# A new order, engines and buffer places for all 908 steps of a fused linear-attention and gated-MLP kernel

## The chip, the cores and the metric

The kernel runs on one core of a Trainium2 chip. The metric is the device time of one execution in microseconds. Five engines work side by side, each through its own list of instructions in order: PE (TensorE, matmuls; its weight loads are shown as PEld), DVE (VectorE), ACT (ScalarE), POOL (GpSimd) and SP (SyncE, which here only issues DMAs). They meet through semaphores.

## What is computed

An attention layer with a decaying state, and behind it a gated MLP whose gate is a cosine:

```python
batch, n_heads, seq, head_dim = (4, 8, 768, 48)
f = 1.0 / (1.0 + np.exp(-f_logit))
for t in range(S):
    state = f[:, :, t, :, None] * state + np.einsum('bhd,bhe->bhde', k[:, :, t], v[:, :, t])
    y[:, :, t] = np.einsum('bhd,bhde->bhe', q[:, :, t], state)
x = y.transpose(0, 2, 1, 3).reshape(B * S, H * D)      # 3072 x 384
h = x @ w_in                                           # 384 x 2048
g = h * np.cos(h)
out = g @ w_out                                        # 2048 x 384
```

## The kernel before

The sequence is cut into 12 pairs of chunks (three pairs to a batch entry, 256 tokens each), and the MLP into 12 units of 256 tokens; unit n works on the output of pair n. All of it is written as a graph of 908 named steps, each of which issues one or a few instructions on one engine. A name is a kind, the number of the pair or unit, and a part:

- f, k, q, v: loads of a pair's inputs (SP, 384 KB; pairs 0 and 1 in halves of 192 KB). w0.i and w1.i: a quarter of w_in and of w_out (768 KB), with wc0.i and wc1.i, the casts to bf16.
- ex, ln, fx, fy, ad, qa, ka: logs of the gates and what goes with them; cum: their running sum on PE; eb and ei: its exponentials on ACT.
- qm and km: q and k times these (lines 492, 503 and 507), on DVE or POOL. tq and tk: their transposes, on PE for pairs 0 to 3 (lines 569 and 575, with the copy qkt out of PSUM) and as DMA transposes issued by SP for the rest (tqn.0, tqn.1, line 558).
- sc: scores on PE (line 595), am: their mask on DVE (line 599, reads the whole of the scores' two PSUM banks). vb and vt: v in bf16 and placed for the products. ps: the outer products of the state (lines 616 and 626), st and sz: the state's sum and decay on DVE (lines 647 and 652). y and yi: the output inside the chunk and from the state (line 680). xe: its copy to bf16.
- hm.js: one eighth of x @ w_in for unit m (line 728, two steps to a block j of 1024 PSUM columns), co: the cosine on ACT (line 733), g: the product on DVE (line 710), which is the last to read the block's two PSUM banks. or.s: a quarter of g @ w_out for row block r (line 744), ot: its copy out of PSUM, out: its DMA.
- zf0 to zf35: 36 matmuls of zeros (line 302) whose result is not used. zqk, zsp, zvt: memsets of buffers.

Nothing is scheduled by the framework. The string ORDER lists all steps; each engine issues its own in that order. A word such as "g0.2:V" or "h0.21:T0" gives the step, the engine (T is PE, V DVE, S ACT, G POOL, Y SP) and the numbers of the buffers that it takes: for PE's results a PSUM bank from 0 to 7 (steps with 1024 columns take two), for others a slot of their pool. A buffer is free for its next user when the last reader of the value in it has run; the semaphore waits follow from that and from what a step reads. SP too runs in order: a DMA whose buffer is not free, or a store whose data is not there, holds up all behind it.

Of the kernel before, what the change touches and what calls it, by code (L numbers as in the profile page):

```python
# [45 lines left out]
tq0.1:T7 ei1.0:S k1.0:Y0 sc0.0:T2 q1.0:Y0 v1.0:Y0 v1.1:Y vb0.0:V1 eb1.0:S0 cum3:T0 vb0.1:V km0.1:G
am0.0:V1 q1.1:Y ei3:S k1.1:Y zf21:T4 zf22:T4 zf23:T6 tk0.1:T qkt0.1:V0 vs0:T4 ps0.1:T6,2 ps0.0:T
vt0.1:V2 eb3:S1 sz0.00:V3 ex1.1:S zf24:T3 zf25:T3 sc0.1:T0 qm1.0:G1 w0.0:Y2 sz0.01:V zf26:T3 zf27:T3
zf28:T3 zf29:T3 sj0.1:T w0.1:Y0 am0.1:V0 vt0.0:S ln1.1:S q2:Y2 ex2:S sz0.10:V2 km1.0:V cum1.1:T4
vb1.1:V1 ei1.1:S km1.1:V vb1.0:S tq1.0:T6 yi0:T0 y0:T7 zf30:T3 zf31:T3 zf32:T3 zf33:T3 zf34:T3  # L50
tk1.1:T1 sz0.11:V tk1.0:T eb1.1:S qm1.1:V zf35:T4 tq1.1:T qkt1.0:V3 sj1.0:T2 xe0.1:S3 vs1:T4 wc0.0:G
# [6 lines left out]
qkt2.0:S4 h1.20:T qkt2.1:V3 km3.0:G sc2.0:T4 km3.1:G h0.31:T v2:Y0 wc1.3:G tq3.0:T3 am2.0:V0 o0.0:T2
vb2:G2 o1.0:T5 co1.2:S1 w1.2:Y2 co0.3:S0 o3.0:T4 o3.1:T vt2.3:G2 tk3.0:T qkt3.0:S2 ex4:S ln4:S0
g1.2:V fx4:S o1.1:T qm3.1:V tq3.1:T7 tk3.1:T g0.3:V o0.1:T sc3.0:T0 qkt3.1:V0 sc3.1:T6 ad4:G2 v3:Y1  # L60
vb3:G0 o0.3:T o2.0:T3 f5:Y0 o2.1:T vt2.0:S k4:Y2 am3.1:V3 am3.0:V1 fy4:S o2.3:T sc2.1:T6 ps2.0:T0
wc1.2:S ps2.1:T st2.00:V st2.01:V vt2.2:S vt2.1:S o3.3:T vt3.1:G0 q4:Y1 o1.3:T k5:Y0 am2.1:V2 v4:Y1
# [16 lines left out]
out2:Y h4.11:T co4.1:S0 st6.11:V g4.2:V vb7:S1 h5.20:T4 h5.21:T g4.3:V ot6:V0 qm7.0:G tq7.0:Y2
km7.1:G sz6.10:V3 h5.10:T2 co5.2:S2 qm7.1:G tq7.1:Y1 q8:Y2 h5.11:T vt6.0:G o7.2:T0 qa6:G co5.1:S1  # L80
qm6.1:G tq6.1:Y3 o7.3:T vt6.3:S g4.1:V o7.0:T sz6.11:V zsp.0:V g5.2:V0 qm6.0:G vt7.1:G0 sc7.0:T4
vt7.0:G g5.1:V ps7.1:T6,7 ex9:S out5:Y ps7.0:T st7.00:V st7.01:V sz7.01:V1 o9.2:T1 sz7.00:V st7.10:V
o9.0:T o7.1:T am7.0:V3 o9.1:T ln9:S0 fy9:S out6:Y st7.11:V sz7.10:V0 fx9:S sz7.11:V ex8:S tq6.0:Y0
o9.3:T vt7.3:G ln8:S1 q9:Y1 k9:Y0 vt7.2:S o8.1:T6 sc6.1:T4 am6.1:V1 sc7.1:T2 vt6.1:G ot9:S0 out9:Y
ad9:G2 cum9:T7 k8:Y2 o8.0:T o8.2:T ad8:G1 cum8:T5 yi7:T1,4 am7.1:V2 y7:T ot7:S3 xe7.1:V0 v8:Y1 fy8:S
qa8:G xe7.0:S sc6.0:T2 eb8:S0 am6.0:V0 o8.3:T k11:Y1 ei8:S2 h7.20:T0 ei9:S1 ka9:G ot8:V0 fx8:S
km9.0:G1 yi6:T5 qa9:G y6:T4 km9.1:G f11:Y3 eb9:S1 qm9.1:G h7.21:T h5.30:T6 h5.00:T2 xe6.0:V3 xe6.1:V
h5.01:T out4:Y h6.00:T4 co7.2:S1 g7.2:V3 co5.0:S2 h5.31:T h6.21:T0 g5.0:V co5.3:S1 g5.3:V vb8:G0
h6.20:T co6.2:S3 h6.01:T co6.0:S1 g6.2:V4 g6.0:V h6.11:T2 h6.10:T h6.31:T6 vt8.1:S0 o11.2:T1
co6.1:S0 v9:Y0 g6.1:V tq9.1:Y2 ka8:G km8.0:G2 qm9.0:G o10.2:T0 out8:Y h6.30:T q11:Y0 co6.3:S1  # L90
h7.10:T4 h7.11:T co7.1:S0 vb9:G1 tq9.0:Y1 o10.3:T o10.1:T g6.3:V o10.0:T o11.1:T qm8.0:G f10:Y2
ex11:S o11.0:T g7.1:V ex10:S ln10:S0 qm8.1:G vt8.0:G vt9.0:S2 ln11:S1 fx11:S out7:Y ot10:V2 sc9.0:T6
v10:Y1 tq8.0:Y0 km8.1:G ps9.1:T0,2 am9.0:V3 sc9.1:T4 am9.1:V1 ps9.0:T sz9.01:V1 sz9.00:V st9.10:V
st9.11:V o12.0:T3 o12.3:T k10:Y0 vt8.3:G o12.1:T o11.3:T ot11:S3 sz9.10:V3 o12.2:T vt9.3:G vt9.1:G
sz9.11:V ad10:G0 fx10:S cum10:T4 eb10:S1 ei10:S0 vt9.2:G tq8.1:Y3 v11:Y2 h7.31:T6 ot12:V0 sc8.0:T0
out12:Y ka10:G km10.1:G1 yi9:T2 y9:T3 xe9.1:V3 h7.30:T am8.0:V1 co7.3:S0 h7.00:T4 g7.3:V o13.1:T2
h7.01:T o13.3:T o13.2:T o13.0:T xe9.0:S vb10:G1 sc8.1:T6 ad11:G1 km10.0:G co7.0:S3 fy11:S g7.0:V
ps8.0:T3 out11:Y ps8.1:T zvt.1:G ps10.1:T0,1 fy10:S ps10.0:T cum11:T4 ei11:S2 am8.1:V3 st8.00:V
st8.01:V sz8.00:V1 o14.2:T5 eb11:S2 sz8.01:V ka11:G vb11:S2 vt8.2:G o14.3:T o14.0:T o14.1:T yi8:T4,7
st10.00:V y8:T qa11:G qm11.0:G2 xe8.0:S1 ot13:V3 km11.1:G h9.21:T2 st10.01:V vt11.2:G2 sz10.00:V2  # L100
h9.20:T xe8.1:V sz10.01:V h8.30:T6 ot14:S0 co9.2:S0 st10.10:V st10.11:V q10:Y2 qm11.1:G sz10.10:V0
qa10:G sz10.11:V g9.2:V1 h8.31:T h8.11:T0 co8.3:S3 h8.21:T4 qm10.1:G tq11.1:Y1 out3:Y g8.3:V4
# [765 lines left out]
```

## Time and profile before

| | |
|---|---|
| time, median of 3 runs | 179.81 us (179.35 to 180.32) |
| the profiled execution | 179.81 us |
| its span, first to last instruction | 177.8 us |
| PE busy | 171.3 us (96%) |
| DVE, ACT, POOL busy | 133.1, 129.8, 98.2 us |
| granted TensorE clock | 1.000 |
| read from and written to HBM | 25.17 MB and 4.72 MB |

The page and the answers of the trace give times in us from the start of the span. A group reads: line, engine, operation, out<-in with the program's buffer names, shapes, count, busy time. In the list of waits a row reads: who waited, for whom, us in total, how often, the longest. In the chain of waits a row is a piece of the path that ended last: its start, its length, what it was. Matmuls are pipelined and their ends are modelled, so neighbours overlap by a little.

### The profile page before, as it was taken

The numbers are of one execution on the slowest core, as the hardware profiler recorded it, in microseconds if no ns is written. First come the engines' busy times: TensorE is split into PE (matmuls) and PEld (weight loads), VectorE is DVE, ScalarE is ACT, GpSimd is POOL, SyncE is SP. The second block draws the span as 40 slices with busy tenths as digits, with TensorE's granted clock in tenths as the row PEclk, the third lists the DMA queues.
The fourth block names the chain that finished last, engine by engine and source line by source line (L and its number), as shares of the span: only waits on it lengthen the run. The fifth ranks groups of instructions, "written<-read, shape, count | busy, mean of one in ns | idle before, by whom it ended". The sixth has DMA issues, their size and how long they took to land.

```text
span 177.8 us, 5968 instructions
## 1 busy us (share of the span) xinstructions
PE 171.3 (96%) x2551; PEld 125.7 (71%) x2554; DVE 133.1 (75%) x208; ACT 129.8 (73%) x177; POOL 98.2 (55%) x125
## 2 busy tenths in 40 slices
PE   7999989999999999999899999999999999999992
PEld 2576768866678867788567886676786767887660
DVE  6299878897696899796997687978878966283710
ACT  3977687759999999778978789989693644464510
POOL 7042569685669989989746988379992000000000
PEclk9999999999999999999999999999999999999999
DMA  4999999999998799997999999991077040000033
GB/s 128 310 307 344 347 352 259 314 307 309 259 243 221 164 245 217 265 232 133 248 173 290 272 204 262 217 264 40 4 162 166 0 177 4 4 12 32 6 130 133
DMA packets 70330, 34.46 MB, mean 194 GB/s; under 512 B 59296, under 2 KB 68768, under 8 KB 70304
## 3 DMA queue, kind: packets, MB, share of 16 engines
q1 hardware_dynamic: 69744, 33.69, 77.8%
q8 instruction: 20, 0.33, 0.8%
q10 hardware_dynamic: 560, 0.39, 0.8%
q14 instruction: 6, 0.05, 0.1%
HBM read 25.17 MB, written 4.72 MB: 168 GB/s over the span
## 4 chain that ended last, share of the span: by engine, by line
PE 87%; DMA 5%; DVE 2%; issue 1%; ACT 1%; SPq 1%; DVEq 0%; ACTq 0%
PE ps L744 34%; PE ps L728 31%; PE ps L680 5%; PE ps L595 4%; DMA out_dram<-ot 3%; PE ps L302 3%; DMA f<-in_f_logit_dram 2%; PE ps L626 1%; DVE g L710 1%; PE ps L569 1%; PE ps L575 1%; PE ps L438 1%; SPq L336 1%; PE ps L424 1%; PE ps L440 1%
## 5 line engine op out<-in xcount | busy, mean ns | idle before, releaser
L710 DVE TENSOR_TENSOR g<-ps,co 128x1024 bf16<-128x1024 f32 x48 | 57.8, 1220 | 18.9 <-ACT co L733 18.1
L744 PE MATMUL ps<-w_out_bf,g 128*128 128x384 bf16 x384 | 68.4, 326 | 0.0
L733 ACT ACTIVATE co<-ps,halfpi 128x1024 bf16<-128x1024 f32 x48 | 52.6, 1112 | 21.6 <-PE ps L728 20.5
L728 PE MATMUL ps<-x,w_in_bf 128*128 128x256 bf16 x576 | 67.4, 273 | 0.0
L728 PEld LDWEIGHTS <-w_in_bf 128*128 128x128 bf16 x576 | 55.4, 98 | 8.5
L744 PEld LDWEIGHTS <-g 128*128 128x128 bf16 x384 | 36.1, 98 | 21.6
L599 DVE TENSOR_TENSOR am<-ps,pmask 128x1024 bf16<-128x1024 f32 x24 | 28.8, 1219 | 5.3 <-PE ps L595 5.0
L787 ACT ACT_TABLE_LOAD x12 | 15.4, 1283 | 1.7 <-PEq L852 1.5
L507 POOL TENSOR_TENSOR qk<-k,bi 128x384 bf16<-128x384 f32 x16 | 16.0, 1000 | 0.6
L507 POOL TENSOR_TENSOR qk<-q,b 128x384 bf16<-128x384 f32 x16 | 15.9, 1001 | 0.6
L197 POOL COPY vt<-vb 64x384 bf16<-64x384 bf16 x27 | 13.5, 501 | 1.3
L410 POOL TENSOR_TENSOR sp<-ls 128x384 bf16<-128x384 f32 x8 | 8.0, 998 | 8.2 <-ACT ls L378 8.1
L197 ACT COPY ot<-ps 128x384 f32<-128x384 f32 (+1 forms) x13 | 5.5, 438 | 9.0 <-PE ps L744 9.0
L197 DVE COPY ot<-ps 128x384 f32<-128x384 f32 (+1 forms) x13 | 6.9, 535 | 6.6 <-PE ps L744 3.5
L302 PE MATMUL ps<-zero 128*128 128x512 bf16 x33 | 10.1, 435 | 1.6 <-DVE zero L203 1.2
L372 ACT ACTIVATE f<-f 128x768 f32<-128x768 f32 (+1 forms) x14 | 10.2, 746 | 1.3 <-DMA f<-in_f_logit_dram 1.3
L595 PE MATMUL ps<-qkt 48*64 48x128 bf16 x384 | 9.4, 220 | 1.4 <-DVE g L710 0.7
L647 DVE TENSOR_TENSOR ps<-ps,sz 128x192 f32<-128x192 f32 x26 | 9.4, 362 | 1.6 <-PE ps L626 0.9
L396 POOL TENSOR_TENSOR k<-k,f 128x384 f32<-128x384 f32 x8 | 8.0, 999 | 4.5 <-DMA k<-in_k_dram 4.5
L595 PEld LDWEIGHTS <-qkt 48*64 48x64 bf16 x384 | 6.3, 106 | 5.1 <-issue 4.3
L197 DVE CAST x<-ps 128x384 bf16<-128x384 f32 x14 | 7.3, 552 | 2.7 <-PE ps L680 2.7
L197 POOL CAST w_in_bf<-g 128x1536 bf16<-128x1536 f32 x4 | 5.9, 1464 | 5.2 <-DMA g<-in_moe_w_in_dram 5.2
(105 smaller groups left out, 189.5 us busy)
## 6 DMA issues: line engine op xcount, KB each, us to landing
out_dram<-ot SPq DMA_DIRECT2D x22, 192.0 KB, 2.6
f<-in_f_logit_dram SPq DMA_DIRECT2D x10, 384.0 KB, 6.7
q<-in_q_dram SPq DMA_DIRECT2D x10, 384.0 KB, 5.3
k<-in_k_dram SPq DMA_DIRECT2D x10, 384.0 KB, 6.7
v<-in_v_dram SPq DMA_DIRECT2D x10, 384.0 KB, 6.1
g<-in_moe_w_in_dram SPq DMA_DIRECT2D x4, 768.0 KB, 8.9
g<-in_moe_w_out_dram SPq DMA_DIRECT2D x4, 768.0 KB, 8.5
q<-in_q_dram SPq DMA_DIRECT2D x4, 192.0 KB, 4.7
```

Of the source, the lines that this page charges most:

```text
L197: (nc.scalar.copy if e == "ACT" else eng(e).tensor_copy)(out=o, in_=i)
L302: G.step(f"zf{i}", ("PE",), lambda e, dump=dump: nc.tensor.matmul(dump.ap, lhsT=zero[:, 0:128], rhs=zero, start=True, stop=True), writes=[ ...
L372: nc.scalar.activation(out=flat(t.ap), in_=flat(t.ap), func=AF.Exp, scale=-1.0)
L507: G.step(f"{nm}{n}.{u}", ("POOL", "DVE") if cut else ("POOL",), lambda e, u=u, j=j, src=src, dec=dec: eng(e).tensor_mul(out=qkp[u][j].ap[: ...
L595: nc.tensor.matmul(o[64 * h:64 * h + 64, r, 2 * a + g, :].rearrange("p (e n) -> p e n", e=2), lhsT=qkv(u)[s, 1, a, g, h, :], rhs=qkv(u)[s, ...
L599: G.step(f"am{n}.{u}", ("DVE",), lambda e, u=u, sc=sc: nc.vector.tensor_mul(out=am[u].ap.rearrange("p r b n -> p (r b) n"), in0=sc.ap.rear ...
L647: G.step(f"st{n}.{g}{r}", ("DVE",), lambda e, r=r, view=view, S0=S0: nc.vector.tensor_add(out=view(), in0=view(), in1=S0.ap[:, :, r, :]), ...
L710: nc.vector.tensor_mul(out=o.rearrange("p b (n e) -> p b n e", e=2), in0=ph.ap.rearrange("p (b e n) -> p b n e", e=2, n=64), in1=co.ap.rea ...
L728: nc.tensor.matmul(ph.ap[:, i * T:(i + 1) * T].rearrange("p (g t) -> p g t", t=C), lhsT=w_in_bf[:, kk, f0:f0 + 128], rhs=xa[:, :, kk, :], ...
L733: G.step(f"co{m}.{j}", ("ACT",), lambda e, ph=ph, co=co: nc.scalar.activation(out=co.ap, in_=ph.ap, func=AF.Sin, bias=halfpi), reads=[ph], ...
L744: nc.tensor.matmul(po.ap[:, 0:DM], lhsT=gT.ap[:, j, i * C:(i + 1) * C], rhs=w_out_bf[:, j, :], start=(po.first and j == 4 * s), stop=(po.f ...
L787: nc.scalar.preload_act_table_set(TABLES[s.table])
```

## The change

ORDER is replaced as a whole, in 78 lines instead of 80, so every line of the new kernel has a number lower by two (line 710 is line 708). No function, no step and no pool size changes; each engine still issues the same kinds of work, PE the same 2554 matmuls. What changes is the order on each engine, the engine of some steps and the buffer of most.

```diff
 ORDER = """
-cqs:G zsp.1:G f0.0:S3 zqk.1:V zsp.2:G f0.1:Y f3:Y0 ex0.0:S ln0.0:S2 ex0.1:S ln0.1:S f1.0:Y1 zqk.2:G
-zvt.2:V q0.0:Y1 k0.0:Y2 cqi:V zf0:T1 zf1:T1 zf2:T1 zf3:T1 zf4:T1 zf5:T1 zf6:T1 zf7:T1 zf8:T2 zf9:T2
...
-h0.21:T0 k3:Y2 g1.1:V3 km2.1:G qm3.0:G2 h0.20:T co1.0:S3 g1.0:V w1.3:Y4 tq2.1:T3 h1.31:T4 h1.30:T
...
+zf9:T2 zf20:T7 zf13:T1 zf28:T4 f0.1:S1 zf15:T3 zqk.1:G f0.0:Y zf2:T1 cqi:V zf16:T2 zf32:T6 ex0.1:S
+zf25:T6 zsp.0:V zf14:T5 zf35:T3 zf24:T2 zf27:T4 ex0.0:S k0.0:Y1 f1.0:Y0 zsp.1:G ln0.0:S1 q1.1:Y2 zqk.0:V
...
+w1.3:Y2 km3.1:G zf10:T6 g1.1:V h0.20:T tq2.0:T2 tk2.0:T km3.0:V v2:Y2 h1.20:T6 co1.3:S1 wc1.0:G g1.3:V
...
```

Three places, as the instructions stand on their engine.

DVE, from the second product g of unit 0 to the mask of a scores block of pair 3; g_154, g_157 and g_155 are the products g of units 0 and 1, qk_124, qk_125 and qk_123 the results of qm and km of pairs 2 and 3. Before:

```order
L710 TENSOR_TENSOR g_154<-ps_169,co_162 128x1024
L710 TENSOR_TENSOR g_157<-ps_170,co_160 128x1024
L710 TENSOR_TENSOR g_157<-ps_172,co_162 128x1024
L710 TENSOR_TENSOR g_154<-ps_169,co_159 128x1024
L710 TENSOR_TENSOR g_157<-ps_171,co_161 128x1024
L197 COPY qkt_140<-ps_170 128x1024
L599 TENSOR_TENSOR am_142<-ps_171,pmask 128x1024
L710 TENSOR_TENSOR g_157<-ps_172,co_160 128x1024
L503 TENSOR_TENSOR qk_125<-q_107,bq_132 128x8x48
L710 TENSOR_TENSOR g_154<-ps_169,co_159 128x1024
L197 COPY qkt_137<-ps_172 128x1024
L599 TENSOR_TENSOR am_145<-ps_172,pmask 128x1024
```

Now:

```order
L708 TENSOR_TENSOR g_157<-ps_170,co_161 128x1024
L501 TENSOR_TENSOR qk_124<-k_103,f_101 128x8x48
L708 TENSOR_TENSOR g_157<-ps_171,co_160 128x1024
L265 MEMSET qk_125 128x32x8
L708 TENSOR_TENSOR g_155<-ps_169,co_162 128x1024
L501 TENSOR_TENSOR qk_123<-k_104,f_100 128x8x48
L597 TENSOR_TENSOR am_142<-ps_171,pmask 128x1024
L501 TENSOR_TENSOR qk_123<-q_107,bq_133 128x8x48
L708 TENSOR_TENSOR g_157<-ps_172,co_161 128x1024
L708 TENSOR_TENSOR g_155<-ps_169,co_159 128x1024
L195 COPY qkt_139<-ps_170 128x1024
L597 TENSOR_TENSOR am_145<-ps_172,pmask 128x1024
```

These are g1.1, km3.0, g1.3, zqk.2, g0.2, km2.1, am2.0, qm2.1, g1.2, g0.3, qkt2.1 and am3.0. Three products with k or q stand on DVE where one stood (qm3.1, now on POOL), a memset came to it, and g1.3 and g0.2 come behind the first product.

SP, the loads of the weights and of pairs 2 and 3; g_... are the places into which the weights are loaded. Before:

```order
L320 DMA g_156<-in_moe_w_in_dram 128x3x512
L320 DMA g_154<-in_moe_w_in_dram 128x3x512
L336 DMA q_108<-in_q_dram 128x8x96
L320 DMA g_157<-in_moe_w_in_dram 128x3x512
L320 DMA g_155<-in_moe_w_in_dram 128x3x512
L336 DMA k_103<-in_k_dram 128x8x96
L336 DMA q_107<-in_q_dram 128x8x96
L320 DMA g_156<-in_moe_w_out_dram 128x4x384
L320 DMA g_155<-in_moe_w_out_dram 128x4x384
L336 DMA k_105<-in_k_dram 128x8x96
```

Now:

```order
L318 DMA g_157<-in_moe_w_in_dram 128x3x512
L318 DMA g_155<-in_moe_w_in_dram 128x3x512
L318 DMA g_158<-in_moe_w_in_dram 128x3x512
L318 DMA g_154<-in_moe_w_in_dram 128x3x512
L334 DMA q_106<-in_q_dram 128x8x96
L334 DMA k_104<-in_k_dram 128x8x96
L334 DMA q_107<-in_q_dram 128x8x96
L334 DMA k_103<-in_k_dram 128x8x96
L318 DMA g_154<-in_moe_w_out_dram 128x4x384
```

The order was w0.0, w0.1, q2, w0.2, w0.3, k2, q3, w1.0, w1.1, k3; it is w0.0, w0.1, w0.3, w0.2, q3, k2, q2, k3, w1.0. The eighteen loads ahead of w0.0 are the same ones in another order in both kernels: all inputs of pairs 0 and 1, f2 and f3.

DVE, where unit 4's products end and unit 5's begin; ot_163 is the copy ot6. Before:

```order
L710 TENSOR_TENSOR g_157<-ps_170,co_162 128x1024
L197 COPY ot_163<-ps_169 128x384
L652 TENSOR_TENSOR sz_149<-ps_169,b_118 128x192
L710 TENSOR_TENSOR g_157<-ps_172,co_159 128x1024
L652 TENSOR_TENSOR sz_149<-ps_169,b_118 128x192
L267 MEMSET sp_112 128x16x8
L710 TENSOR_TENSOR g_154<-ps_171,co_161 128x1024
```

Now:

```order
L708 TENSOR_TENSOR g_154<-ps_172,co_161 128x1024
L708 TENSOR_TENSOR g_154<-ps_170,co_162 128x1024
L645 TENSOR_TENSOR ps_169<-ps_169,sz_148 128x192
L650 TENSOR_TENSOR sz_149<-ps_169,b_117 128x192
L708 TENSOR_TENSOR g_156<-ps_171,co_161 128x1024
```

The rows are g4.3, ot6, sz6.10, g4.1, sz6.11, zsp.0, g5.2 before, and g4.1, g4.3, st6.11, sz6.11, g5.2 now. ot6 stands on ACT now. Its buffer was last used by ot2, and is last used by ot3 now.

On PE, the steps with small shapes (sc, ps, vs, y, yi) stand between others in 28 runs before and in 26 now.

More of the change, by code (lines that the diff above doesn't have):

```diff
@@ L46 @@
[L46 to L51, printed above, removed]
@@ L58 @@
[L58 to L62, printed above, removed]
@@ L79 @@
[L79 to L102, printed above, removed]
```

109 lines of the change are left out of this document (71 added, 38 removed).

## The prediction

> **What bounds the kernel now.** First the page's busy times, then the whole core by stretches (each row: the stretch, its length, busy time and count of PE, PEld, DVE, ACT and POOL, granted clock, DMA share, GB/s), then who PE waited for.
>
> ```profile
> PE 171.3 (96%) x2551; PEld 125.7 (71%) x2554; DVE 133.1 (75%) x208; ACT 129.8 (73%) x177; POOL 98.2 (55%) x125
> 1.19:25.87 24.68, 23.53 (x423) 15.31 (x427) 18.59 (x50) 18.97 (x32) 10.18 (x18) 1.00 1.02 313
> 25.87:43.00 17.13, 17.13 (x202) 13.62 (x196) 14.92 (x15) 12.18 (x13) 13.90 (x13) 1.00 1.09 298
> 43.00:85.00 42.00, 42.00 (x707) 31.81 (x705) 35.05 (x59) 38.60 (x54) 35.77 (x44) 1.00 1.01 221
> 85.00:86.00 1.00, 0.28 (x10) 0.21 (x12) 1.00 (x2) 0.98 (x2) 0.90 (x3) 1.00 1.01 264
> 86.00:174.50 88.50, 88.41 (x1228) 64.72 (x1226) 62.81 (x83) 58.81 (x80) 36.90 (x46) 1.00 0.60 132
> PE ps L302 <- DVE zero L203: 1.2, 1, 1.2
> PE ps L595 <- DVE g L710: 0.7, 1, 0.7
> ```
>
> PE is the bound: from 25.87 us on it is never idle but for 0.7 us at 85, where a scores block (L595) waits for the product g (L710) that still reads its bank. Before 25.87 it is idle for 24.68 - 23.53 = 1.15 us. The change keeps all 2554 matmuls, the 36 zero fillers among them, so it can only move idle time of PE, and put new waits in. The sum is made against the profiled execution, 179.81 us, which is also the median of the three runs; 177.8 of it is the span.
>
> The loads are the second limit: the DMA share is full until 85, and in the first stretches every load lands in the order of its issue. The timeline of POOL (start, length, instruction, in brackets the wait and what ended it) shows when:
>
> ```profile
> 21.45 1.47 POOL L197 CAST w_in_bf<-g 128x1536 bf16<-128x1536 f32 x1 [0.69 <-DMA g<-in_moe_w_in_dram]
> 25.52 1.46 POOL L197 CAST w_in_bf<-g 128x1536 bf16<-128x1536 f32 x1 [0.94 <-DMA g<-in_moe_w_in_dram]
> 32.88 1.46 POOL L197 CAST w_out_bf<-g 128x1536 bf16<-128x1536 f32 x1 [0.66 <-DMA g<-in_moe_w_out_dram]
> 35.07 1.47 POOL L197 CAST w_out_bf<-g 128x1536 bf16<-128x1536 f32 x1 [0.72 <-DMA g<-in_moe_w_out_dram]
> 36.90 1.95 POOL L503 TENSOR_TENSOR qk<-k,f 128x384 bf16<-128x384 f32 x2 [0.37 <-DMA k<-in_k_dram]
> ```
>
> A weight piece of 768 KB takes 35.07 - 32.88 = 2.19 us. k3, a piece of 384 KB, takes 36.90 - 35.07 = 1.83; between 25.52 and 32.88 land two weight pieces and two of 384 KB (w0.3, k2, q3, w1.0), so (7.36 - 4.38) / 2 = 1.49 each.
>
> **Part 1, up to the first full run of L728 (h0.10), 25.87 us before.** The same work stands ahead of h0.10 in both orders, except that one filler (0.22 us) now comes behind it. The chain of waits shows the largest loss there:
>
> ```profile
> 22.08 0.68 PE ps L728 x6
> 22.75 0.23 PE ps L595 x5
> 22.98 0.64 issue
> 23.62 0.37 PE ps L595 x9
> 35.51 0.35 PE ps L595 x16
> ```
>
> The scores of pair 1 took 0.23 + 0.64 + 0.37 = 1.24 us, where a scores block takes 0.35: they stood behind a product of DVE that had their bank. In the new order both scores blocks come ahead of h0.01 with DVE's am products between other work. What can go is the 1.15 us of idle time, the rest of the stretched block (1.24 - 0.35 - 0.64 = 0.25), and the filler, 1.6 us together. Against it: k1.1 is the last load ahead of the weights in both orders, and its product km1.1 goes from DVE to POOL:
>
> ```profile
> 17.34 0.56 DVE L492 TENSOR_TENSOR qk<-k,f 128x384 bf16<-128x384 f32 x1
> 14.67 1.00 POOL L492 TENSOR_TENSOR qk<-q,bq 128x384 bf16<-128x384 f32 x1 [2.05 <-DMA q<-in_q_dram]
> ```
>
> That is 0.44 us later for the transposes that wait for it, of which I keep 0.2, since fillers stand there. Gain of part 1: 1.4 us, between 0.8 and 1.8. h0.10 then starts at 24.5.
>
> **Part 2, 24.5 to about 43 us.** DVE gets three products of pairs 2 and 3 (km3.0, km2.1, qm2.1) in place of one (qm3.1), and km3.0 stands ahead of g1.3 and g0.2, which free PSUM for PE. It waits for k3. SP's new order puts q3, k2, q2 and k3 ahead of all of w_out. By 32.88 - 2.19 = 30.69 us all of w_in, q2, k2 and q3 had landed before, and the bytes ahead are the same now, so k3 lands 1.49 to 1.83 later: 32.2 to 32.5, I take 32.4. What follows on DVE:
>
> ```profile
> 38.18 1.09 DVE L503 TENSOR_TENSOR qk<-q,bq 128x384 bf16<-128x384 f32 x1
> 42.04 2.36 DVE L599 TENSOR_TENSOR am<-ps,pmask 128x1024 bf16<-128x1024 f32 x2 [0.55 <-PE ps L595]
> ```
>
> Such a product takes 0.56 (L492, POOL idle) to 1.09 (L503, POOL at k3's products from 36.90 to 38.85); POOL works on pair 3 here too, so 1.0. Two ops of 128x1024 take 2.36, so 1.15 apart. g0.2 ends at 32.4 + 1.0 + 1.15 (g1.3) + 0.2 (a memset, put on DVE there) + 1.15 = 35.9, and h0.30 writes the bank that it reads: PE starts h0.30 at 36.0. PE would come there at
>
> ```profile
> 31.57 1.31 PE ps L728 x12
> 32.88 0.67 PE ps L575 x12
> ```
>
> 24.5 + twelve h blocks of 0.655 (7.9) + six transpose blocks of 0.22 (1.3) + one scores block with its change of shape (0.45) + the filler (0.22) = 34.3. So it waits 1.7 us. Before, g0.2 was the last of these four, ended at 33.70, and PE did not wait:
>
> ```profile
> 28.54 5.16 DVE L710 TENSOR_TENSOR g<-ps,co 128x1024 bf16<-128x1024 f32 x4 [0.62 <-ACT co L733]
> ```
>
> Bounds: 0.9 if k3 lands at 31.9 and km3.0 takes 0.56; 2.4 if it lands at 32.7 and km3.0 waits out a product of POOL. Behind it, o3.0 waits for am2.0, tq2.1 for qm2.1 and sc2.1 for qkt2.1, all in DVE's unbroken queue: 0.35 us (0 to 1.0).
>
> **Part 3, 43 us to the end.** The wait at 85 has its cause here:
>
> ```profile
> 76.55 1.41 SPq L755 DMA_DIRECT2D out_dram<-ot  x1
> 82.40 0.56 DVE L197 COPY ot<-ps 128x384 f32<-128x384 f32 x1 [1.35 <-DMA out_dram<-ot]
> 84.68 2.29 DVE L710 TENSOR_TENSOR g<-ps,co 128x1024 bf16<-128x1024 f32 x2
> ```
>
> DVE stood 1.35 us for out2, issued late behind two loads, before it could copy ot6, and so ended g5.2 after PE had come to sc7.0. In the new order ot6 goes to ACT, and it takes the place of ot3, whose store out3 stands eighteen steps of SP ahead of out6. Gain 0.8 (0.7 by the row of PE's waits, and the scores behind).
>
> PE's blocks of small shape (scores, outer products, y) stand in 26 runs instead of 28. A run costs at its borders:
>
> ```profile
> 136.46 0.57 PE ps L595 x32
> 137.03 0.76 PE ps L744 x4
> 104.44 1.30 PE ps L744 x8
> ```
>
> 0.76 - 0.65 = 0.11 on the way out, about as much on the way in, so 0.2 for a run. One of the two goes in part 1, whose 1.6 us of loss already holds it; that leaves 0.2 here. New waits: at y4, yi4, h4.21 and h7.21 the new order leaves DVE's queue, counted in the durations above, about as long as PE's work beside it; I put 0.1 us on each of the four, 0.4 us (0 to 1.2), as an estimate.
>
> The last copies change engines (DVE then ACT instead of ACT then DVE) and stay one behind the other:
>
> ```profile
> 174.44 0.32 ACT L197 COPY ot<-ps 128x192 f32<-128x192 f32 x1 [2.12 <-PE ps L744]
> 174.79 0.36 DVE L197 COPY ot<-ps 128x192 f32<-128x192 f32 x1 [1.69 <-ACT ot L197]
> ```
>
> So nothing there. **Sum:** -1.4 + 1.7 + 0.35 - 0.8 - 0.2 + 0.4 = +0.05: **179.9 us**.
>
> **Rivals.**
> *The waits of part 2 are short.* PE itself is gapless there now, and each number that makes the wait leans on k3's landing. With k3 at 31.9, km3.0 at 0.56 and the low ends behind: -1.6 + 0.9 + 0.1 - 0.8 - 0.2 + 0.1 = -1.5: 178.3 us. For it: all of the early gain is idle time that the rows show; against it: the sum of landed bytes.
>
> *DVE's three products wait out POOL's work (slower).* The row of 1.09 began at 38.18, with POOL at work until 38.85, and ended at 39.27, 0.42 behind it: it looks like a wait for POOL's end and then the work. POOL's neighbours now are casts of 1.46 us. If km3.0 meets a product of 1.00 and one of the other two a cast, they take 1.56 and 2.02 instead of 1.0 and 1.0, in an unbroken queue on which PE already waits: +1.6, 181.5 us. It decides once the three take over 4 us together. The Trainium skill, SBUF — State Buffer, Who interferes with whom, says that a DVE instruction with two SBUF inputs contends with a GpSimd instruction that reads SBUF, and that the later one blocks fully until the other is through. By that rule this rival's mechanism is right, and only who comes first is open; the trace agrees at 38.18 (1.09 against 0.56), and has no row of such a product against a cast.
>
> *The transposes of pair 8 come late (slower).* SP issues q8 right behind tq9.1, and tq8.1 and tq8.0 further on; before, q8 stood ahead of all transposes of pairs 6, 8 and 9. The page's list of issues (count, size, median us to landing) and SP's timeline:
>
> ```profile
> q<-in_q_dram SPq DMA_DIRECT2D x10, 384.0 KB, 5.3
> qkt<-qk SPq DMA_TRANSPOSE x16, 3.8
> 100.14 2.70 SPq L558 DMA_TRANSPOSE qkt<-qk  x1
> 104.36 2.24 SPq L558 DMA_TRANSPOSE qkt<-qk  x1
> ```
>
> From q8's issue: 5.3 + 1.0 (qa8) + 1.0 (qm8.1) + 3.8 (tq8.1) + 2.5 (SP's time for tq8.0 behind it) = 13.6 us, and the issue is 3.8 - 2.5 = 1.3 ahead of tq9.1's landing. PE has from sc9.1 to sc8.0 thirteen blocks of 0.65 and nine small ones of some 2.3 together, 10.8 us. So if tq9.1 lands just as PE wants it, sc8.0 waits 13.6 - 1.3 - 10.8 = 1.5 us: 181.4 us. It decides from a lead of tq9.1 under 1.5 us; against it speaks that POOL is busy for only 36.90 of 88.50 us after 86, so qa8 and the product behind it need not queue.
>
> **How the numbers follow.** The forecast 44%; short waits 28%; POOL's lock 17%; pair 8 late 11%. A difference under 0.5% (0.9 us) is about what a measurement here can't tell from none: faster 0.28, same 0.44, slower 0.28. The range runs from the first rival's time to just over the second's, 178.3 to 181.7; the forecast's own is 179.0 to 180.8.
>
> **What would show it.** Right: the first run of L728 blocks on PE starts near 24.5; DVE idle for 1 to 2 us until a k load lands at 32 to 33, with PE idle for 1 to 2 us between 33 and 37; nothing at sc7. Wrong: PE gapless to 43 (first rival); DVE rows of L501 at 1.5 us and more (second); PE waiting for a transpose DMA past 115 us (third). A load order that is not landed in issue order would make part 2 wrong as a whole.

## The result: 3.3% slower, and the profile after

| | before | after |
|---|---|---|
| time, median | 179.96 us (179.35 to 180.32, 4 runs) | 185.49 us (185.10 to 187.53, 4 runs) |
| ratio to the kernel before, 95% interval | | 1.033 (1.025 to 1.041) |
| the profiled execution, its span | 179.81, 177.8 us | 185.4, 183.6 us |
| last matmul of PE ends | 174.4 us | 180.2 us |
| the first full run of L726 blocks (h0.10; L728 before) starts | 25.87 us | 27.70 us |

The forecast was 179.9 us, between 178.3 and 181.7. In the profiles of a_three, a_six and mix_km3 below, PE's clock fell after a long stop and their spans are longer by that; the ratios leave out the slower runs (5 of 10 of a_three, 4 of 9 of a_six, 3 of 8 of a_four, 3 of 12 of mix_mended, at most 2 of any other, almost none of the kernel before), so they put these kernels rather too low.

First the page's busy times of the changed kernel, then its core by stretches that hold about the same work as the four shown before (the stretch, its length, busy time and count of PE, PEld, DVE, ACT and POOL, granted clock, DMA share, GB/s):

```profile
PE 171.9 (94%) x2554; PEld 125.7 (68%) x2554; DVE 135.4 (74%) x218; ACT 127.8 (70%) x172; POOL 98.6 (54%) x120
1.19:27.70 26.51, 23.29 (x425) 15.32 (x426) 17.59 (x51) 18.25 (x31) 10.98 (x15) 1.00 0.91 275
27.70:47.00 19.30, 18.31 (x234) 14.08 (x227) 17.51 (x19) 13.29 (x13) 15.28 (x15) 1.00 1.07 300
47.00:89.00 42.00, 40.44 (x671) 30.74 (x669) 34.93 (x57) 37.56 (x53) 32.65 (x40) 1.00 1.10 234
89.00:180.20 91.20, 89.90 (x1237) 65.57 (x1234) 64.68 (x90) 58.36 (x76) 39.15 (x48) 1.00 0.56 122
```

PE's matmuls are the same. Its idle time is 26.51 - 23.29 = 3.22, then 0.99, 1.56 and 1.30 us, 7.07 in all, where it was 1.15, 0, 0.72 and 0.09, 1.96 in all. So 5.1 of the 5.8 us by which PE ends later is new idle time, and it lies in all four stretches; where the other 0.7 comes from was not followed. And in the first stretch the DMA share is 0.91, where it was 1.02: the loads, the second limit, were not kept busy. Who PE waited for (in all, how often, the longest):

```profile
PE ps L593 <- DMA qkt<-qk: 2.7, 3, 1.6
PE ps L454 <- issue: 1.2, 1, 1.2
PE ps L300 <- DVE zero L201: 1.2, 1, 1.2
PE ps L529 <- DVE vq L518: 1.1, 1, 1.1
PE ps L567 <- POOL qk L490: 0.8, 1, 0.8
PE ps L726 <- DVE g L708: 0.4, 1, 0.4
PE ps L742 <- DVE am L597: 0.3, 1, 0.3
PE ps L573 <- DVE qk L501: 0.2, 1, 0.2
```

Only the third row is old. L529, L567 and L454 lie in the start (vs0, tk1.1, cum2); L726, L742 and L573 are h0.30, o3.0 and tq2.1, the places of the prediction's second part; L593 are scores blocks that wait for DMA transposes: sc5.1, sc7.1 and sc11.0. The old wait at sc7.0 is not among them.

**The start.** SP's queue shows what the forecast had not looked for (start, length, instruction; f, q, v, k are the tiles loaded):

```profile
7.71 0.61 SPq L334 DMA_DIRECT2D f<-in_f_logit_dram  x1
8.36 1.05 SPq L334 DMA_DIRECT2D q<-in_q_dram  x1
11.44 0.60 SPq L334 DMA_DIRECT2D v<-in_v_dram  x1
```

From 9.41 to 11.44 SP stands still. The next load is v1.1. In the order before, v0 was in place 2 of v and v1 in place 0; now both are in place 0, so v1.1 waits for the last reader of v0, vb0.0 on DVE, which ends at 11.41. First the loads of v1 on SP before, which waited for nothing, then vb0.0 on DVE now:

```profile
10.21 1.27 SPq L336 DMA_DIRECT2D v<-in_v_dram  x2
```

```profile
10.80 0.61 DVE L518 TENSOR_SCALAR vq<-v,odd 128x768 bf16<-128x768 f32 x1
```

Every load behind it slides: k1.1 lands at 19.18 instead of 17.26, w0.0 at 22.55 instead of 19.24, and k3 at 34.58, where the forecast had 32.4.

**The middle.** DVE, from the product that waits for k3 (in brackets the wait and what ended it):

```profile
34.60 1.21 DVE L501 TENSOR_TENSOR qk<-k,f 128x384 bf16<-128x384 f32 x1 [0.39 <-DMA k<-in_k_dram]
35.73 1.21 DVE L708 TENSOR_TENSOR g<-ps,co 128x1024 bf16<-128x1024 f32 x1
36.95 0.27 DVE L265 MEMSET qk<- 128x256 uint32 x1
37.14 1.16 DVE L708 TENSOR_TENSOR g<-ps,co 128x1024 bf16<-128x1024 f32 x1
38.22 1.36 DVE L501 TENSOR_TENSOR qk<-k,f 128x384 bf16<-128x384 f32 x1
39.51 1.21 DVE L597 TENSOR_TENSOR am<-ps,pmask 128x1024 bf16<-128x1024 f32 x1
40.64 1.06 DVE L501 TENSOR_TENSOR qk<-q,bq 128x384 bf16<-128x384 f32 x1
```

This is the chain of the prediction: k3, km3.0, g1.3, the memset, g0.2 (ends at 38.30), and h0.30 starts at 38.35.

**The rest.** From the chain of work that ended last (start, length, what it was), around pair 5 and pair 11:

```profile
69.77 4.42 DMA qkt<-qk
74.20 0.04 issue
74.24 0.64 PE ps L593 x32
...
139.95 1.00 POOL qk L505
140.95 0.04 issue
140.99 0.46 POOLq L861
141.45 4.61 DMA qkt<-qk
146.10 0.86 PE ps L593 x48
```

Before either scores block PE had been idle since its last matmul: 1.6 us ahead of 74.24, 0.8 ahead of 146.10.

### The profile page after: what moved, and what is told of

It is laid out like the page before. It is cut to its first block, busy times and chain, and to the rows that moved or that the text cites. A ratio compares the mean times of both kernels' runs of the same rounds, so it can differ in the third digit from the quotient of the medians.

```text
span 183.6 us, 5978 instructions
## 1 busy us (share of the span) xinstructions
PE 171.9 (94%) x2554; PEld 125.7 (68%) x2554; DVE 135.4 (74%) x218; ACT 127.8 (70%) x172; POOL 98.6 (54%) x120
## 4 chain that ended last, share of the span: by engine, by line
PE 42%; DMA 23%; POOL 11%; ACT 7%; issue 6%; SPq 5%; DVE 4%; POOLq 0%; ACTq 0%
PE ps L742 20%; PE ps L726 15%; DMA qkt<-qk 7%; DMA g<-in_moe_w_in_dram 6%; POOL qk L505 5%; DMA k<-in_k_dram 5%; SPq L334 4%; DMA q<-in_q_dram 3%; ACT co L731 3%; PE ps L678 3%; DMA v<-in_v_dram 2%; PE ps L593 2%; DVE qk L501 2%; ACT vt L195 1%; DVE g L708 1%
## 5 line engine op out<-in xcount | busy, mean ns | idle before, releaser
L742 PE MATMUL ps<-w_out_bf,g 128*128 128x384 bf16 x384 | 68.7, 326 | 0.3 <-DVE am L597 0.3
L726 PE MATMUL ps<-x,w_in_bf 128*128 128x256 bf16 x576 | 67.5, 273 | 0.4 <-DVE g L708 0.4
L726 PEld LDWEIGHTS <-w_in_bf 128*128 128x128 bf16 x576 | 55.7, 98 | 9.4 <-issue 0.5
L742 PEld LDWEIGHTS <-g 128*128 128x128 bf16 x384 | 36.1, 98 | 21.9 <-issue 0.5
L195 DVE COPY ot<-ps 128x384 f32<-128x384 f32 (+1 forms) x17 | 8.6, 517 | 9.1 <-PE ps L742 9.0
L195 ACT COPY ot<-ps 128x384 f32<-128x384 f32 (+1 forms) x9 | 4.1, 456 | 14.8 <-PE ps L742 13.6
L384 POOL TENSOR_TENSOR q<-f,q 128x384 f32<-128x384 f32 x8 | 8.0, 1000 | 8.2 <-DMA q<-in_q_dram 4.0
L300 PE MATMUL ps<-zero 128*128 128x512 bf16 x36 | 11.1, 434 | 1.2 <-DVE zero L201 1.2
L593 PE MATMUL ps<-qkt 48*64 48x128 bf16 x384 | 8.5, 220 | 3.0 <-DMA qkt<-qk 2.7
L593 PEld LDWEIGHTS <-qkt 48*64 48x64 bf16 x384 | 6.2, 106 | 6.2 <-DMA qkt<-qk 4.0
L195 DVE CAST x<-ps 128x384 bf16<-128x384 f32 x16 | 8.2, 550 | 0.8 <-PE ps L678 0.7
```

The costliest lines, as they stand in the source:

```text
L195: (nc.scalar.copy if e == "ACT" else eng(e).tensor_copy)(out=o, in_=i)
L300: G.step(f"zf{i}", ("PE",), lambda e, dump=dump: nc.tensor.matmul(dump.ap, lhsT=zero[:, 0:128], rhs=zero, start=True, stop=True), writes=[ ...
L593: nc.tensor.matmul(o[64 * h:64 * h + 64, r, 2 * a + g, :].rearrange("p (e n) -> p e n", e=2), lhsT=qkv(u)[s, 1, a, g, h, :], rhs=qkv(u)[s, ...
L726: nc.tensor.matmul(ph.ap[:, i * T:(i + 1) * T].rearrange("p (g t) -> p g t", t=C), lhsT=w_in_bf[:, kk, f0:f0 + 128], rhs=xa[:, :, kk, :], ...
L742: nc.tensor.matmul(po.ap[:, 0:DM], lhsT=gT.ap[:, j, i * C:(i + 1) * C], rhs=w_out_bf[:, j, :], start=(po.first and j == 4 * s), stop=(po.f ...
```

## The experiments

All edits are words of ORDER; what isn't named stays as it was. Ratios are to the kernel before, timed beside each.

**1. The shared place of v, taken away from the new order.**

```diff
-v1.1:Y0
+v1.1:Y1
```

> The changed kernel, with the loads of v of pair 1 (v1.0, v1.1) in a place of their own instead of the place of pair 0's v. Theory A (the early loss comes from SP: v1.1 waits 2.0 us, 9.42 to 11.44, for vb0.0 on DVE to read pair 0's v out of that place, and every later load slides with it): v1.1 is issued at about 9.5, k1.1 lands at about 17.2 instead of 19.18, k3 at about 32.6 instead of 34.58, h0.10 starts at about 26 instead of 27.70, and the time falls by 1.5 to 2.2 us, to 183.3 to 184.0. Theory B (the early loss comes from the new order on PE and DVE, of which vs0's wait of 1.1 us is a part, and the loads only follow): the loads come 2 us earlier, but h0.10 moves by less than 0.7 us and the time by less than 0.7.

Ratio 1.019 (1.014 to 1.023) instead of 1.033, median 183.23 us: 2.3 us faster, just past theory A's 1.5 to 2.2. SP's queue now:

```profile
8.36 1.15 SPq L334 DMA_DIRECT2D q<-in_q_dram  x1
9.56 0.62 SPq L334 DMA_DIRECT2D v<-in_v_dram  x1
```

The stop is gone, w0.0 lands at 20.31 and k3 at 32.47. But h0.10 starts at 27.54, only 0.16 earlier, which is theory B's number. The gain comes later: h0.30 starts 0.9 us earlier, sc5.1 1.8. So the shared place made the loads late, and the late loads cost in the middle and in the rest; the start has another loss beside it.

**2. The shared place alone, put into the old order.** A first try placed v of pair 1 over that of pair 0 ahead of its readers:

```diff
-v1.0:Y0 v1.1:Y vb0.0:V1 ... vb0.1:V
+v1.0:Y2 v1.1:Y vb0.0:V1 ... vb0.1:V
```

> The kernel before, with this one part of the change: v of pair 1 is loaded into the place of pair 0's v. Theory A (the shared place alone makes the early loss): SP waits from 10.2 to about 11.8 for vb0.1, every later load lands 1.5 us later, and the time rises by 1.0 to 1.7 us, to 180.9 to 181.6. Theory B (the old order has room for loads that come 1.5 us later, and the new order has not, or the loss is elsewhere): the time rises by less than 0.5 us.

Here pair 0 is computed from pair 1's v, and its readers wait for that later load: ratio 1.038, which says nothing on the question. With the loads behind the readers:

```diff
-v1.0:Y0 v1.1:Y vb0.0:V1 ... vb0.1:V
+vb0.0:V1 ... vb0.1:V v1.0:Y2 v1.1:Y
```

> The kernel before, with this one part of the change: v1.0 and v1.1 are loaded into the place of pair 0's v, after its readers. Theory A (the shared place alone makes the early loss): SP waits from 10.2 to about 11.8 for the second reader of pair 0's v, every later load lands 1.5 us later, and the time rises by 1.0 to 1.7 us, to 180.4 to 181.1. Theory B (the old order has room for loads that come 1.5 us later): the time rises by less than 0.5 us.

Ratio 1.011 (1.001 to 1.020). SP stood from 10.14 to 11.86 and k3 landed at 38.91 instead of 36.83. The profiled span is 178.5, 0.7 us over the old one. So there is a cost, but its size is open between 0.2 and 3.7 us by the interval: theory A's 1.0 to 1.7 lies in it, and theory B's under 0.5 is not ruled out.

**3. The two halves apart.** Up to h0.10 one order, behind it the other (the places of the first part renumbered so that what lives over the border lies where the second part has it).

> All steps that stand ahead of h0.10 in the order before, in that order, on those engines and in those places (renumbered where the rest needs it); behind them all other steps in the new order. Theory A (the two halves add up: the start costs 1.8 to 2.3 us, the rest of the new order costs what a_v1_own showed of it, 0.5 at tq2.1, 1.1 at sc5.1, 0.3 at sc9.1, 1.2 at sc11.0, less the 0.9 of the wait at sc7.0 that goes): h0.10 starts at 25.9, and the time is 181.0 to 182.0. Theory B (the rest of the new order loses only because its loads come late: with the old start's loads its waits shrink to under 1 us in all): 179.0 to 180.2, the wait at sc11.0 excepted. Theory C (the start doesn't matter, PE gets back to the same place by the loads behind it): 183.0 or more.

> The other way round: all steps that stand ahead of h0.10 in the new order, in it; behind them all others in the order before. Theory A (the halves add up): h0.10 starts at about 27.7, the rest runs without waits but for sc7.0, and the time is 181.0 to 182.2. Theory B (the old rest too loses more when its loads come 2 us late): 182.5 to 184.5. Theory C (the old rest has room and catches up): 180.3 or less.

mix_old_start: 1.012 (1.008 to 1.015); h0.10 starts at 25.55. mix_new_start: 1.013 (1.004 to 1.023); h0.10 at 27.38. Theory A in both: each half costs about 2 us (0.012 and 0.013 of 180), 4.4 together, where the whole loses 6.0 (0.033). By the intervals alone the 1.6 between could be noise. The profiles say that the halves aggravate each other: from h0.10 to PE's end the new rest takes 150.2 us behind the old start and 152.5 behind the new one; the old rest takes 148.5 and 148.8. PE's waits with the old start in front of the new rest are two rows:

```profile
PE ps L593 <- DMA qkt<-qk: 2.4, 3, 1.1
PE ps L300 <- DVE zero L201: 1.2, 1, 1.2
```

With k3 landed at 31.64 there is no wait at h0.30, o3.0 or tq2.1: the second part's wait is k3's. The transposes stay late.

**4. The transposes of pairs 5 and 11, one at a time.**

```diff
-out3:Y ... k6:Y0 ... tq5.0:Y2 ... tq5.1:Y1
+... tq5.0:Y2 ... tq5.1:Y1 out3:Y k6:Y0
```

> The changed kernel, with the two transposes of pair 5 (tq5.0, tq5.1) issued on SP ahead of the store out3 and the load k6. Theory A (sc5.1's wait of 1.6 us at 72.6 comes from the queue: qm5.1 is ready at 67.0, but the transposes stand behind v5, out3 and k6 and land only at 73.3 and 74.2): tq5.1 lands at 72.7 or earlier, sc5.1 waits at most 0.3 us, and the time falls by 1.1 to 1.6 us, to 183.9 to 184.4. Theory B (the loads are the limit here, and what comes later, k6 with the transposes of pair 6 behind it, brings the wait back further on): sc5.1's wait goes, but the time falls by less than 0.5 us.

```diff
-co8.3:S1 fy11:S
+fy11:S co8.3:S1
```

> The changed kernel, with fy11 ahead of the cosine co8.3 on ACT instead of behind it. Theory A (sc11.0's wait of 1.2 us at 144.9 comes from there: co8.3 waits for g9.2 to free its place, fy11 stands behind it until 134.17, POOL waits 3.1 us for fy11 before qa11, and so qm11.0 and the transpose tq11.0 come late): qa11 starts at about 132.3 instead of 134.76, tq11.0 lands by 144, sc11.0 doesn't wait, and the time falls by 0.7 to 1.2 us, to 184.3 to 184.8. Theory B (the transposes of pairs 10 and 11, one behind the other on SP, or POOL's other work set it): sc11.0 still waits 0.7 us or more and the time stays within 0.4 us of 185.5.

a_tq5_first: 1.029 (1.024 to 1.033), median 184.52, 1.0 us less. sc5.1 does not wait. But from h0.10 to the end PE takes 152.4 us as in the changed kernel (152.5): sc7.1, sc6.1, sc9.1 and sc11.0 wait more. By the mechanism that is theory B, though the time fell by more than its 0.5: the 1.1 us by which PE ends earlier stand in this profile's start. a_fy11_first: 1.034 (1.028 to 1.040). qa11 starts at 132.42 and sc11.0 does not wait, as theory A has it, but the time did not follow. In its profile PE takes 1.1 us less from h0.10 on; the start is 0.6 us later, with a stop in cum2 of 2.0 us instead of 1.2. One wait at a time tells little here: the profiles of the same start scatter by 1 us.

**5. All of them together.**

> The changed kernel with three edits at once: v1 in a place of its own, tq5.0 and tq5.1 ahead of out3 and k6 on SP, fy11 ahead of co8.3 on ACT. Theory A (the three waits are apart, and each gain stays): 185.5 - 2.3 - 1.0 - 0.2 to 1.0 for the wait at sc11.0, so 181.2 to 182.0. Theory B (once the loads come earlier, the transposes of pair 5 and of pair 11 are no longer late, or the next load takes the gain back): 182.6 to 183.4.

> The changed kernel with v1 in a place of its own, tq5.0 and tq5.1 ahead of out3 and k6, q9 ahead of out9 and f11, fy11 ahead of co8.3. Only the new start is left as it is. Theory A (start and rest add up): the waits at sc5.1, sc9.1 and sc11.0 are gone, h0.10 starts at about 27.5, and the ratio is 1.005 to 1.011. Theory B (with this start the loads stay late, and the waits come back elsewhere): 1.014 or more.

a_three: 1.009 (1.003 to 1.014), 181.5 us by this ratio, which is theory A's; but the median of all its runs, 183.02, would be theory B's, and its profile has a new stop of PE of 2.3 us, which the last section takes up. a_four, with the load q9 ahead of out9 and f11 besides: 1.007 (1.003 to 1.011), median 181.67, h0.10 at 26.76, no wait at sc5.1, sc9.1 or sc11.0; waits for transposes of 0.8 us at sc7.1 and 0.2 at sc6.1 stay. So four edits make up 4.7 of the 6.0 us by the ratios (1.033 to 1.007): theory A.

> The old start with the rest of the new order (as in mix_old_start), and three edits in the rest: tq5.0 and tq5.1 ahead of out3 and k6 on SP, the load q9 ahead of out9 and f11, fy11 ahead of co8.3 on ACT. Theory A (the three waits of the rest, 1.2 at sc5.1, 0.4 at sc9.1, 1.3 at sc11.0, have these causes and are apart): none of the three is over 0.3 us, PE ends at 172.9 to 173.4 instead of 175.70, and the time is 1.0 to 1.5 us under the kernel before, a ratio of 0.991 to 0.995. Theory B (the waits move on to the next load or transpose): the ratio is 1.000 or more.

The same edits of the rest behind the old start: 1.002 (0.999 to 1.005), theory B by its number. The three waits are gone, but PE ends at 174.66, not at 173.4: this profile's start was 0.9 us later than mix_old_start's (h0.10 at 26.48) and h0.30 waited 0.4. From h0.10 to the end it takes 148.2 us, the old kernel 148.5. So the rest of the new order, with these faults mended and behind the old start, is as good as the old one, no better.

**6. The gain of the third part alone, in the old order.**

```diff
-out1:Y ... out2:Y
+out1:Y out2:Y ...
```

> The kernel before, with the store out2 issued right behind out1 on SP (at about 60 instead of 76.5), so that ot6 need not wait for it. Theory A (the wait at 85 has its cause there, and the 0.8 us of the prediction's third part are real): ot6 no longer waits 1.35 us, sc7.0 waits less than 0.2, and the time falls by 0.6 to 0.9 us, to 0.995 to 0.997 of the kernel before. Theory B (sc7.0 is held by the transposes or by DVE's queue all the same, or the store delays the loads behind it): the wait at 85 stays above 0.4 us and the ratio within 0.002 of 1.

Ratio 1.002 (0.999 to 1.004): theory B. DVE at ot6 and g5.2, and PE at sc7.0 (start, length, instruction):

```profile
81.86 0.55 DVE L197 COPY ot<-ps 128x384 f32<-128x384 f32 x1
84.42 2.35 DVE L710 TENSOR_TENSOR g<-ps,co 128x1024 bf16<-128x1024 f32 x2
```

```profile
86.00 0.42 PE L595 MATMUL ps<-qkt 48*64 48x128 bf16 x16
```

ot6 has no wait and sc7.0 none. Yet sc7.0 starts at 86.00, where it started at 85.89: this profile's start was 0.34 us later, and a new stop of PE of 0.45 us stands at 76.60. That stop needs no edit of out2: b_v1_shared, which has none, stops 0.36 us at the same matmul. What the twelve runs show is that the end of the wait at 85, alone, is worth nothing that can be measured.

**7. What is left of the start.** Ten profiles of the new start have a stop inside cum2, the step whose matmuls compute the running sums of pair 2. PE before, and after:

```profile
22.68 0.30 PE L595 MATMUL ps<-qkt 48*64 48x128 bf16 x5
23.62 0.37 PE L595 MATMUL ps<-qkt 48*64 48x128 bf16 x11 [0.64 <-issue]
```

```profile
23.74 0.17 PE L451 MATMUL ps<-far,ident 128*128 128x8 bf16 x1
25.12 0.24 PE L454 MATMUL ps<-half,sp 128*128 128x4 bf16 x4 [1.22 <-issue]
```

Both stops lie between matmuls of one step, where nothing is waited for ("issue"). Counted in the trace, one is at PE's 352nd weight load and the other at its 353rd, though the steps that stand there differ. The 0.64 of before is the row that the prediction read as a bank held by DVE. Three edits went at it and at vs0:

```diff
-q1.1:Y2 ... km0.1:V1 vb0.0:V ... q1.0:Y
+vb0.0:V km0.1:V1 ... q1.0:Y2 q1.1:Y
```

> The changed kernel with v1 in a place of its own, and in the start the load q1.1 (of pair 1, fourth on SP) behind q1.0 and vb0.0 ahead of km0.1 on DVE. Theory A (what is left of the start's loss begins with vs0, which waits 0.6 to 1.3 us because a load of pair 1 stands ahead of six of pair 0 and a product ahead of vb0.0): vs0 waits less than 0.3 us, h0.10 starts 0.6 to 1.2 us earlier than the 27.5 of a_v1_own, and the ratio falls from its 1.0185 to 1.012 to 1.015. Theory B (k1.1, the last load ahead of the weights, and PE's stop in cum2 set h0.10, so that an earlier vs0 only waits further on): vs0's wait goes, but h0.10 stays within 0.4 us of 27.5 and the ratio within 0.003 of a_v1_own's.

1.019 (1.015 to 1.024), a_v1_own's ratio: theory B for the time. vs0 waits under 0.3 us and h0.10 starts at 26.45, where theory A has it, but the stop grew to 1.4 us and from h0.10 on PE took 151.0 us.

```diff
-zf22:T2 tq1.0:T0 ... zf5:T3 ... zf7:T2 zf0:T1 zf19:T3 tk1.0:T ... tq1.1:T7 tk1.1:T
+tq1.0:T0 ... tk1.0:T ... tq1.1:T7 zf22:T2 zf5:T3 zf7:T2 zf0:T3 zf19:T2 tk1.1:T
```

> a_four with five of PE's zero fillers (zf22, zf5, zf7, zf0, zf19; 0.22 us each) moved from ahead of tk1.0 to ahead of tk1.1, where PE waits for km1.1 anyway; no load and no other engine changes. Theory A (PE's stop at its 352nd weight load is its code that comes a set time, some 5.8 us, after PE has passed a place near its 228th; the fillers then pass that place 0.8 us earlier and reach the 352nd at the same time): the stop shrinks from 1.04 to under 0.4 us, h0.01 and h0.10 start 0.6 to 0.9 earlier than in a_four, tk1.1 at the same time as there. Theory B (the stop is a wait for data or a buffer that is late by the loads): it stays at 0.9 us or more, and h0.10 is no earlier.

1.012 (1.004 to 1.021). The stop stayed at 1.2 us, theory B's number; but PE now waited at tk1.0 and cum3, so it passed its 228th weight load only 0.2 us earlier (18.35 instead of 18.56), and the test did not tell the two apart.

> a_four_fill with q1.1 behind q1.0 on SP and vb0.0 ahead of km0.1 on DVE. Theory A (shared place, vs0, the stop and the late transposes are the whole loss): vs0 waits under 0.3 us, the stop is under 0.4, h0.10 starts at 25.3 to 26.2, and the ratio to the kernel before is 0.996 to 1.003. Theory B (something else in the new order costs too): 1.006 or more.

1.008 (1.004 to 1.013): theory B, a_four's ratio within the intervals. vs0 does not wait, the stop is 1.3 us. The last one moves the same five fillers to the end of PE's program:

> a_four with the five fillers zf22, zf5, zf7, zf0, zf19 at the very end of PE's program instead of in the start. Ahead of cum2 PE then has five weight loads fewer. Theory A (the stop belongs to the place in PE's program): PE again stops 0.5 us or more at its 352nd or 353rd weight load, which is now inside the block of L726 behind cum2 (h0.01), and cum2 runs through without a stop. Theory B (it belongs to cum2, a wait for its data or its bank): the stop stays inside cum2, at the 346th to 348th. Either way h0.10 comes 0 to 0.8 us earlier than the 26.8 to 27.3 of a_four and a_four_fill.

```profile
23.36 0.24 PE L454 MATMUL ps<-half,sp 128*128 128x4 bf16 x4
23.46 0.27 PE L726 MATMUL ps<-x,w_in_bf 128*128 128x256 bf16 x1
24.73 1.03 PE L726 MATMUL ps<-x,w_in_bf 128*128 128x256 bf16 x8 [1.00 <-issue]
```

cum2 runs through, and PE stops inside h0.01, at its 353rd weight load again: theory A. The stop belongs to the place in PE's program and not to a step's data. The ratio is 1.009 (1.005 to 1.012): five fillers fewer gain nothing, since PE waits at vs0 (0.9 us) and cum3 (0.7) instead.

**8. km3.0 behind g1.3 and g0.2.**

```diff
-tk2.0:T km3.0:V ... tk3.0:T sc2.0:T4 qkt3.0:S1 ... g0.2:V ... h0.31:T
+tk2.0:T ... sc2.0:T4 ... g0.2:V km3.0:V ... h0.31:T tk3.0:T qkt3.0:S1
```

> mix_mended with km3.0 behind g0.2 on DVE, and on PE tk3.0, which reads it, behind h0.31. Theory A (h0.30 waits, as predicted, for g0.2 behind km3.0, whose 1.2 to 1.4 us beside POOL stand ahead of g1.3 and g0.2): h0.30 starts 0.5 to 0.9 us earlier against h0.10 (10.3 us behind it in mix_mended), no wait takes its place, and the ratio to the kernel before is 0.995 to 1.000. Theory B (the wait moves to sc3.0 or tq2.1, or the gain is lost further on): h0.30 comes earlier but the ratio stays at 1.001 or more.

h0.30 starts 9.64 us behind h0.10 instead of 10.32 and doesn't wait: the mechanism is the predicted one. The time is theory B's, 1.010 (1.005 to 1.016):

```profile
39.27 0.97 PE L742 MATMUL ps<-w_out_bf,g 128*128 128x384 bf16 x5 [1.19 <-ACT qkt L195]
```

o1.0 takes the bank of tk3.0, which this edit moved right ahead of it, and so waits for the copy qkt3.0. The wait that went was 0.4 us, the one that came 1.2; this profile has the new stop of PE as well, 2.6 us (last section).

## Why the prediction was wrong

**Part 1 failed** (-1.4 predicted, +1.83 measured at h0.10). Its step was "k1.1 is the last load ahead of the weights in both orders", with the landing times of before. It compared the order of the loads and not the places that they are loaded into, though the change renumbers these too; v1 in v0's place held SP for 2.0 us. Second, it counted 0.64 us of stopped PE as a bank wait that a new order removes. It is a stop at a fixed place in PE's program, and no bank is waited for; it went from 0.64 to 1.22, and with all loads mended (a_four) it is still 1.0. Third, vs0 waited 1.1 us for the product of v, which the forecast did not price. The 0.2 put down for km1.1 on POOL fits where the loads are mended (a wait of 0.25 at tk1.1 in a_four); with k1.1 1.9 us later it was 0.8. Over all profiles h0.10 starts at 25.55 to 26.74 with the old start (five, mean 26.2), at 26.64 to 28.27 with the new one (four, mean 27.5), and at 26.45 to 27.54 with the new one and v1 in a place of its own (seven, mean 27.0).

**Part 2 was right in its mechanism.** Predicted were 1.7 us at h0.30 and 0.35 behind it; against a_three, where PE waits at none of these steps, it lost 0.2 us at sc2.0, 0.5 at h0.30, 0.5 at o3.0 and 0.3 at tq2.1, 1.5 in all. With the 1.83 of part 1 and the 2.05 of part 3 that is 5.4 of the 5.8 us. The wait was shorter than forecast because PE came late as well: k3 landed 6.9 us behind the start of h0.10, where the forecast had 32.4 - 24.5 = 7.9, and h0.30 started 10.65 behind it instead of 11.5. In a_fy11_first, where k3 landed 8.6 behind, it was 11.7. The estimate of k3's landing, 32.4, holds where SP doesn't wait: 32.47 in a_v1_own. km3.0 took 1.21 where 1.0 was put. mix_km3 shows that it is the place of km3.0 that makes h0.30 wait, and mix_old_start that nothing waits if k3 comes at 31.6.

**Part 3 failed in the other direction**: -0.6 predicted, +2.05 measured (idle time of PE from 47 us on, 1.56 + 1.30 against 0.72 + 0.09), and its places were wrong. sc7.0 no longer waits, but sc7.1 waits for its transpose in the same stretch, and b_out2_early puts the worth of the wait's end alone between a gain of 0.1% and a loss of 0.4%: the 0.8 us were a wait's length taken for a gain. None of the four places put down for new waits (y4, yi4, h4.21, h7.21) waited. Three others did: sc5.1, sc9.1 and sc11.0, 1.6 + 0.1 + 0.8 us; the forecast had looked for new waits on DVE's queue and for late transposes at pair 8 alone. The 0.2 for two runs of small shapes fewer was not tested apart.

**The rivals.** "Short waits" did not come. "Pair 8's transposes late" named the right kind of wait at the wrong pair: sc8.0 did not wait, the pairs 5, 9 and 11 did, behind a store and a load on SP (5), a late load of q (9), and POOL's wait for fy11 (11); pair 7 waited 0.3, and why was not followed. The sign that it named, PE waiting for a transpose past 115 us, did come, at 146. The forecast followed one pair's load; the question had to be put for every pair. "DVE's products wait out POOL" was right in its mechanism and too high in its price. In mix_mended first POOL's product, then DVE's two of the same size:

```profile
32.83 1.01 POOL L501 TENSOR_TENSOR qk<-k,f 128x384 bf16<-128x384 f32 x1
```

```profile
32.91 1.35 DVE L501 TENSOR_TENSOR qk<-k,f 128x384 bf16<-128x384 f32 x1
36.67 0.54 DVE L501 TENSOR_TENSOR qk<-k,f 128x384 bf16<-128x384 f32 x1
```

The first began 0.08 us behind POOL's and ended 0.42 behind its end, the second ran with POOL idle: 1.35 against 0.54. That agrees with the rule of the Trainium skill, SBUF — State Buffer, Who interferes with whom, that the later one is blocked until the other is through. In the changed kernel POOL ran these beside DVE's three:

```profile
33.43 1.96 POOL L501 TENSOR_TENSOR qk<-q,bq 128x384 bf16<-128x384 f32 x2 [0.41 <-DMA q<-in_q_dram]
37.71 1.46 POOL L195 CAST w_out_bf<-g 128x1536 bf16<-128x1536 f32 x1 [1.04 <-DMA g<-in_moe_w_out_dram]
39.83 1.47 POOL L195 CAST w_out_bf<-g 128x1536 bf16<-128x1536 f32 x1 [0.65 <-DMA g<-in_moe_w_out_dram]
```

They end at 35.39, 39.17 and 41.30, and DVE's products 0.40 to 0.42 us behind each, at 35.81, 39.58 and 41.70. So all three waited POOL out, a cast as well as a product; but they had begun when only a part of POOL's work was left, and took 1.21 + 1.36 + 1.06 = 3.63 us, under the 4 from which the rival was to decide.

What stays open is how the 0.8 us between the new start with mended loads and the old one (means of 27.0 and 26.2) divide between the stop, vs0 and the load order, since profiles of one start scatter by as much; and what the shared place costs in the old order, beyond that it costs.

## What to carry to other kernels

When an order is replaced, list for every load not only what stands ahead of it but whose place it takes and which instruction frees that place: a renumbered buffer is a new wait, and in a queue that issues in order one wait delays everything behind it. Loads that come 2 us late need not hurt where they are late; with v1 in a place of its own PE won 0.2 us at h0.10, 0.9 at h0.30 and 1.8 at sc5.1, 47 us behind h0.10. And a wait removed from an engine that is busy 96% of the time is not yet time gained: put it to the test alone first.
